# A gated mix of a state-space convolution and a GELU layer: start of the loads, time steps spread by a product, twelve warming products, due times from a table

## The chip, the core and the metric

The kernel runs on one core of a Trainium2 chip. The metric is the device time of the kernel in microseconds (us), the median of some runs. The core has a matrix engine (TensorE, PE in the profile; the loads of its weights are PEld), a vector engine (VectorE, DVE), a scalar engine (ScalarE, ACT), GpSimd (POOL), a queue that issues transfers (SyncE, SP), and 16 DMA engines. Each engine works through its own instructions in the order of the program and waits at semaphores for the others.

## The reference

```
dt = exp(log_dt);  A = A_re + i A_im;  B, C likewise          # 512 channels x 128 states
K[d, l] = Re sum_n C[d,n] * exp(dt[d] * A[d,n] * l) * dt[d] * B[d,n]     # 2048 taps
a = causal convolution of u with K (by FFT) + u * Dskip       # 2048 x 512
b = gelu(x @ w1 + b1) @ w2 + b2,  x = u                       # 512 -> 1792 -> 512
g = sigmoid(sum(x * gate_w))                                  # one value per row
out = g * a + (1 - g) * b
```

## The kernel before

The program has two parts. `front` makes three streams of work at once. `dense` is the GELU layer: 64 steps: two passes, one for each half of w1's columns, over 8 blocks of 256 rows, four steps to a block; in a step one or two groups f of 128 columns of w1 are multiplied with the rows (L904 to L906, three products of 256 columns for each of four parts, because each float is split in a high and a low part), ScalarE makes the GELU (L921) and the high part (L924), VectorE the low part (L931), and the output products with w2 follow (L947 to L950). `taps` computes the convolution's kernel: for four groups u of 128 channels and four chunks c of each it builds powers and waves on VectorE and ScalarE, contracts them on TensorE (L709, 16 groups of 128 small products), and applies a first stage of a transform (L428), whose results go to memory (L751). `signal` applies the first stage (L428, too) to the input. Then `conv` reads both back, multiplies them in the frequency domain (L1140, L1179), and writes the result (L1295 on).

What `front` does is created as tasks, each with an engine, a duration, a due time and the tasks that it depends on. `Plan.run` goes through them like a simulator with the planner's own durations: each time an engine is free it takes, among the tasks that are ready at that moment, the one with the lowest due time (a task that needs another table of ScalarE counts `TABLE` more). The instructions are then emitted in that order, which is the order in which each engine and each queue works on the chip. Before the change the due times are formulas of the step with tuned constants (`T_0`, `T_MLP`, `K_0`, `T_KG`, `D_...`).

At the start, SP loads the first block of x in two halves (L801), `log_dt` (L504), then the pieces of w1 and w2 of 256 KB each (L1008), the biases and `prm` (L538). Each half of x and each piece is split in a high part (L806 or L808) and a low one (L810). A hidden product needs both halves of x and its piece of w1, split. TensorE starts with `warm`: `N_WARM` products of a tile of zeros (L1025), then two products (L1029) that spread the row b2 and the row gate_w over the 128 partitions.

The time steps dt take this way: `log_dt` is loaded as 128 x 4, VectorE and ScalarE compute exp (L488 to L501), SP stores the result to memory (L508), and GpSimd's queue reads it back, spread over all partitions (L540), before VectorE multiplies the parameters with it (L546). With that multiplication the taps begin.

## Time and profile before

| | us |
|---|---|
| runs: median (lowest to highest of 3) | 510.12 (509.39 to 512.53) |
| the profiled execution's own time | 510.31 |
| its span in the profile | 508.3 |
| TensorE busy in the span | 500.2 |
| VectorE busy | 430.0 |
| ScalarE busy | 364.7 |

The profiled execution's time is its span and 2.01 us around it. Busy time of an engine is the union of its instructions. Rows of a timeline give start, duration, engine, line, operation, tiles and shapes, and in brackets the idle time before and what ended it.

### The profile page before, as it was taken

To read this page: it belongs to the slowest core of one execution; us is meant where nothing else is said; L and a number is where in the kernel's file an instruction comes from. 1 tells how busy PE (TensorE), PEld (TensorE's weight loads), DVE (VectorE), ACT (ScalarE), POOL (GpSimd) and SP (SyncE) were. 2 spreads that over 40 slices of the span, in tenths; PEclk is the share of its full clock that TensorE was granted. 3 is DMA by queue.
4 is the path that set the end of the run, shared out by engine and by line. 5 is a ranking of instruction groups with operands and counts; after the bars stand their busy time and mean duration, and the time that the engine had idled before them with its cause. 6 is when DMAs were issued, how large, how long until landed. Compare 5 with 4: busy or idle time off the path is not lost.

```text
span 508.3 us, 12156 instructions
## 1 busy us (share of the span) xinstructions
PE 500.2 (98%) x4792; PEld 382.8 (75%) x4792; DVE 430.0 (85%) x814; ACT 364.7 (72%) x631; POOL 39.6 (8%) x80
## 2 busy tenths in 40 slices
PE   9999999999999999999998999999999999999996
PEld 6998788898989888788887898998898832222452
DVE  5797999999999999999998989999950188777546
ACT  5799997889999599999766998738634455565300
POOL 1000000000000000001020010120010000231100
PEclk9999999999999999999999999999999999999999
DMA  8977597732558642789594233951478899989997
GB/s 269 327 250 269 156 258 236 225 128 66 149 120 260 193 165 64 207 241 239 142 269 139 86 54 59 218 119 29 144 179 206 201 368 401 376 300 399 324 339 294
DMA packets 81552, 107.60 MB, mean 212 GB/s; under 512 B 39396, under 2 KB 43880, under 8 KB 80952
## 3 DMA queue, kind: packets, MB, share of 16 engines
q1 hardware_dynamic: 74936, 82.81, 51.6%
q0 software_dynamic: 6176, 21.80, 16.1%
q10 hardware_dynamic: 384, 2.23, 1.3%
q8 instruction: 37, 0.61, 0.5%
q14 instruction: 19, 0.16, 0.1%
HBM read 61.19 MB, written 45.62 MB: 210 GB/s over the span
## 4 chain that ended last, share of the span: by engine, by line
PE 74%; ACT 16%; DMA 4%; SPq 3%; issue 2%; DVE 1%; DVEq 0%; POOL 0%; ACTq 0%; POOLq 0%
PE pk L709 10%; PE ph L904 8%; PE acc L947 7%; PE ph L905 7%; PE ph L906 7%; PE acc L948 7%; PE acc L950 7%; PE p2u L1140 5%; PE p2k L1140 5%; PE pa L1179 3%; PE pb L1295 3%; ACT ph L921 2%; PE ph L428 2%; ACT L921 2%; SPq L751 1%
## 5 line engine op out<-in xcount | busy, mean ns | idle before, releaser
L904 PE MATMUL ph<-xh,wh 128*128 128x256 f32 x448 | 129.4, 289 | 0.5 <-ACT attic L446 0.5
L905 PE MATMUL ph<-xlo,wh 128*128 128x256 f32 x448 | 128.1, 286 | 1.5 <-issue 1.5
L906 PE MATMUL ph<-xh,wl 128*128 128x256 f32 x448 | 127.9, 285 | 0.0
L904 PEld LDWEIGHTS ph<-xh,wh 128*128 128x128 f32 x448 | 86.4, 193 | 9.3 <-issue 5.4
L905 PEld LDWEIGHTS ph<-xlo,wh 128*128 128x128 f32 x448 | 86.5, 193 | 3.5 <-issue 1.7
L906 PEld LDWEIGHTS ph<-xh,wl 128*128 128x128 f32 x448 | 86.4, 193 | 0.0
L947 PE MATMUL acc<-wh,hh 128*128 128x512 f32 x209 | 84.2, 403 | 0.0
L948 PE MATMUL acc<-wl,hh 128*128 128x512 f32 x209 | 82.2, 393 | 0.0
L950 PE MATMUL acc<-wh,hl 128*128 128x512 f32 x209 | 81.8, 392 | 0.0
L921 ACT ACTIVATE ph<-ph,b1t 128x256 f32<-128x256 f32 x112 | 50.4, 450 | 38.9 <-PE ph L906 37.1
L709 PE MATMUL pk<-y,den 128*32 128x64 f32 x2048 | 61.4, 290 | 0.0
L709 PEld LDWEIGHTS pk<-y,den 128*32 128x32 f32 x2048 | 57.2, 136 | 3.3 <-issue 1.8
L931 DVE TENSOR_TENSOR hl<-ph,hh 128x512 fp32r<-128x512 f32 (+1 forms) x62 | 38.3, 620 | 22.6 <-ACT hh L924 22.2
L947 PEld LDWEIGHTS acc<-wh,hh 128*128 128x128 f32 x209 | 39.3, 188 | 17.4 <-issue 7.8
L950 PEld LDWEIGHTS acc<-wh,hl 128*128 128x128 f32 x209 | 39.3, 188 | 8.8
L671 DVE TENSOR_TENSOR y<-y,ea 128x64 f32<-128x64 f32 (+4 forms) x80 | 45.4, 567 | 0.1
L948 PEld LDWEIGHTS acc<-wl,hh 128*128 128x128 f32 x209 | 39.3, 188 | 6.4
L516 DVE TENSOR_TENSOR loft<-den,zz 128x256 f32<-128x256 f32 (+2 forms) x48 | 37.4, 778 | 0.5
L517 DVE TENSOR_TENSOR loft<-den,zz 128x256 f32<-128x256 f32 (+2 forms) x48 | 37.3, 776 | 0.0
L1148 ACT COPY k<-p2k 128x512 f32<-128x512 f32 x32 | 18.7, 586 | 25.4 <-issue 10.2
L684 DVE TENSOR_TENSOR y<-y,loft 128x2048 f32<-128x2048 f32 x16 | 36.6, 2288 | 0.2
L924 ACT CAST hh<-ph 128x512 fp32r<-128x512 f32 (+1 forms) x62 | 33.0, 533 | 2.4 <-PE acc L948 0.2
(200 smaller groups left out, 875.0 us busy)
## 6 DMA issues: line engine op xcount, KB each, us to landing
tk_d<-sk SPq DMA_DIRECT2D x32, 256.0 KB, 5.0
t_d<-sa SPq DMA_DIRECT2D x32, 256.0 KB, 5.1
tu_d<-attic SPq DMA_DIRECT2D x40, 128.0 KB, 2.8
attic<-in_xt_dram SPq DMA_DIRECT2D x16, 256.0 KB, 5.4
xh_d<-xh SPq DMA_DIRECT2D x8, 512.0 KB, 4.5
xl_d<-xlo SPq DMA_DIRECT2D x8, 512.0 KB, 5.0
attic<-in_xs_dram SPq DMA_DIRECT2D x16, 256.0 KB, 5.3
out_dram<-io SPq DMA_DIRECT2D x16, 256.0 KB, 3.3
```

Of the source, the lines that this page charges most:

```text
L516: vec(2 * m, lambda: vv.tensor_mul(t, a, br), due, [ka, *kb], [kt])
L671: nc.vector.tensor_mul(both(n, 64 - 3 * n, n), both(0, 64 - n, n), an)
L709: nc.tensor.matmul(pks[q][32 * j : 32 * j + 32, :, gg], x[:, r, :, ch], y[:, r, :, ch], start=(r == 0), stop=(r == 1), skip_group_check=True,)
L904: nc.tensor.matmul(p, h, xh[xk][:, d], start=(d == 0), stop=False)
L905: nc.tensor.matmul(p, h, xlo[xk][:, d], start=False, stop=False)
L906: nc.tensor.matmul(p, lo, xh[xk][:, d], start=False, stop=(d == 3))
L921: nc.scalar.activation(phs[q][:, n], phs[q][:, n], AF.Gelu_apprx_tanh, bias=b1t[:, f : f + 1])
L931: nc.vector.tensor_sub(lo, phs[q][:, 0:nf], hi.bitcast(F32))
L947: nc.tensor.matmul(a, h, wh[1][w], start=start, stop=False, skip_group_check=seeded)
L948: nc.tensor.matmul(a, h, wl[1][w], start=False, stop=False, skip_group_check=seeded)
L950: nc.tensor.matmul(a, l, wh[1][w], start=False, stop=stop, skip_group_check=seeded)
L1140: nc.tensor.matmul(out[64 * i : 64 * i + 64], w, x, start=True, stop=True)
```

## The change

- SP's first loads are the second half of x, w1[0] and the first half of x. `log_dt` goes to GpSimd's queue.
- For the first 128 channels dt isn't read back from memory: a 0/1 matrix (`some`, 32 x 128, new columns of `c1`, loaded by GpSimd's queue) is scaled by dt on VectorE, a product with ones on TensorE spreads it over the partitions, and VectorE copies it to `dtb`. The store to memory stays, for the other three groups.
- `N_WARM` is 12 instead of 8.
- The due times of all 1,539 tasks are replaced by the entries of a table, `DUES`, one for each task in the order of creation; they are ranks, not times. The formulas and their constants (changed, too) now set only the order of creation. The planner's idea of early transfers changes (1.5 times as long in its first 6.5 us, 2.6 us instead of 1.2 to the end of one on GpSimd's queue).

`conv` is not touched. Counted in the order of creation, the lowest entries of SP's loads are: second half of x 0, w1[0] 1, first half 2, w1[1] 4, w1[4] 6, w2[1] 7, w1[3] 13, b1 16, w1[2] 18, w1[5] 19, w1[6] 22, w2[6] 23, w2[0] 25, w2[2] 32, `prm` 53. GpSimd's queue: b2 0, `log_dt` 2, gate_w 3, `some` 8, c1 9. TensorE: warm 0, the product that spreads dt 3, the first hidden product 6, the one that spreads b2 26, the one for gate_w 33.

```diff
-T_0 = 36.21
-T_MLP = 409.57
-K_0 = 25.82
-T_KG = 357.09
+T_0 = 36.61
+T_MLP = 402.64
+K_0 = 24.02
+T_KG = 346.19
...
-TABLE = 21.3
+TABLE = 8.48
...
-N_WARM = 8
+N_WARM = 12
...
+DUES = """
+2 48 1704 7 63 0 8 101 3 31 2 0 9 1 25 4 7 18 32 13 55 6 75 19 64 22 23 16 3 0 3 1 0 26 460 580 33 1539 174
...
+"""
...
     c1 = np.tile(np.stack([er, ei], 2).reshape(32, 64), (4, 1))
+    some = np.arange(P)[:, None] == np.arange(P) // 4
+    c1 = np.concatenate([c1, some], 1)
...
-                dma = max(dma, at + 1.2) + t.done
-                end = dma + 1.2
+                dma = max(dma, at + 1.2) + t.done * (1.5 if dma < 6.5 else 1.0)
+                end = dma + (1.2 if p == "SP" else 2.6)
...
-            move(2, lambda: nc.sync.dma_start(x, logdt.rearrange(shape, c=4)), D_DT, [], ["dt"])
+            move(2, lambda: nc.gpsimd.dma_start(x, logdt.rearrange(shape, c=4)), -300, [], ["dt"], queue="GP")
...
-            move(2, lambda: nc.sync.dma_start(dt_d.rearrange(shape, c=4), r), -200, ["dt"], ["dt_d"])
+            move(2, lambda: nc.sync.dma_start(dt_d.rearrange(shape, c=4), r), D_SD, ["dt"], ["dt_d"])
+            some, scaled, ones = (x4[0:32, 0, k] for k in range(3))
+            pl.add("POOL", 0.1, lambda: nc.gpsimd.memset(ones, 1.0), -190, [], ["x4"])
+            move(16, lambda: nc.gpsimd.dma_start(some, c1[0:32, 64:192]), -190, [], ["x4"], queue="GP")
+            vec(
+                UW,
+                lambda: v.tensor_mul(
+                    scaled.rearrange("p (a b) -> p a b", b=4),
+                    some.rearrange("p (a b) -> p a b", b=4),
+                    r[0:32].unsqueeze(1).to_broadcast([32, 32, 4]),
+                ),
+                -190, ["dt"], ["x4"],
+            )
+            mm(
+                0.4, lambda: nc.tensor.matmul(pus[1][:, 0:UW], ones, scaled, start=True, stop=True), -190,
+                ["x4"], [("pu", 1)], tiled=True,
+            )
+            vec(UW, lambda: v.tensor_copy(dtb, pus[1][:, 0:UW]), -190, [("pu", 1)], ["dtb"])
...
-            move(
-                200, lambda: nc.gpsimd.dma_start(dtb, dt_d[:, sl].to_broadcast([P, UW])), t - 20 if u else -97,
-                ["dt_d"], ["dtb"], queue="GP",
-            )
+            if u:
+                move(
+                    200, lambda: nc.gpsimd.dma_start(dtb, dt_d[:, sl].to_broadcast([P, UW])), t - 20,
+                    ["dt_d"], ["dtb"], queue="GP",
+                )
...
-                lambda: nc.gpsimd.dma_start(c1t, c1),
+                lambda: nc.gpsimd.dma_start(c1t, c1[:, 0:64]),
...
+        for t, due in zip(pl.tasks, map(float, DUES.split()), strict=True):
+            t.due = due
         for t in pl.run():
```

## Rows read from the trace of the kernel before

**Rows 1.** The page: span, busy time by engine, TensorE's granted clock in 40 slices.

```profile
span 508.3 us, 12156 instructions
...
PE 500.2 (98%) x4792; PEld 382.8 (75%) x4792; DVE 430.0 (85%) x814; ACT 364.7 (72%) x631; POOL 39.6 (8%) x80
...
PEclk9999999999999999999999999999999999999999
```

**Rows 2.** Busy time by stretch: length, each engine's busy us (instructions), clock, DMA.

```profile
0.00:8.41 8.41, 7.42 (x20) 4.54 (x20) 2.61 (x9) 3.71 (x6) 2.29 (x10) 1.00 0.68 210
8.41:13.47 5.06, 5.06 (x24) 5.06 (x24) 4.20 (x13) 3.53 (x5) 0.00 (x0) 1.00 1.07 383
13.47:402.90 389.43, 386.74 (x4254) 337.51 (x4252) 349.14 (x676) 314.17 (x539) 26.01 (x52) 1.00 0.62 173
402.90:503.98 101.08, 100.99 (x498) 35.72 (x497) 73.18 (x117) 43.30 (x82) 11.32 (x18) 1.00 0.96 350
```

**Rows 3.** Timeline of TensorE, the first 14 us: start, us, line.

```profile
0.99 3.79 PE L1025 MATMUL acc<-dm 128*128 128x128 f32 x16 [0.99 <-POOL dm L1019]
4.71 2.06 PE L1029 MATMUL acc<-io,s 1*128 1x512 f32 x2
6.57 1.91 PE L1029 MATMUL pu<-io,s 1*128 1x512 f32 x2
8.41 0.58 PE L904 MATMUL ph<-xh,wh 128*128 128x256 f32 x1
...
13.06 0.42 PE L904 MATMUL ph<-xh,wh 128*128 128x256 f32 x1
13.27 0.36 PE L905 MATMUL ph<-xlo,wh 128*128 128x256 f32 x1
...
13.58 0.28 PE L904 MATMUL ph<-xh,wh 128*128 128x256 f32 x1
13.70 0.29 PE L905 MATMUL ph<-xlo,wh 128*128 128x256 f32 x1
```

**Rows 4.** Timeline of SP's queue, the first issues.

```profile
0.74 0.87 SPq L801 DMA_DIRECT2D attic<-in_xt_dram  x2
1.66 0.42 SPq L504 DMA_DIRECT2D dts<-in_logdt_dram  x1
2.13 0.91 SPq L1008 DMA_DIRECT2D sk<-in_w_dram  x2
```

**Rows 5.** Timelines of ScalarE, VectorE, SP and GpSimd: w1's first piece, then dt.

```profile
7.09 0.62 ACT L808 CAST wh<-sk 128x512 fp32r<-128x512 f32 x1 [2.05 <-DMA sk<-in_w_dram]
7.74 0.69 DVE L810 TENSOR_TENSOR wl<-sk,wh 128x512 fp32r<-128x512 f32 x1 [1.37 <-ACT wh L808]
10.28 0.16 DVE L501 TENSOR_TENSOR dts<-dts,dts 128x4 f32<-128x4 f32 x1
10.54 0.33 SPq L508 DMA_DIRECT2D dt_d<-dts  x1
15.65 0.54 POOL L540 DMA_DIRECT2D dtb<-dt_d  x1 [12.46 <-DMA dt_d<-dts]
24.51 0.68 DVE L546 TENSOR_TENSOR pr<-pr,dtb 128x512 f32<-128x512 f32 x1
```

**Rows 6.** Waits of TensorE over the whole span: total, times, longest.

```profile
PE ph L905 <- issue: 1.5, 1, 1.5
...
PE ph L904 <- ACT attic L446: 0.5, 1, 0.5
```

**Rows 7.** The chain that ended last, around the start of `conv`: start, us, what.

```profile
394.77 7.46 DMA tk_d<-sk
405.16 4.12 DMA cc<-in_c_dram
415.61 1.72 PE p2k L1140 x8
```

**Rows 8.** Timeline of TensorE: the first products of `conv` on the taps.

```profile
406.41 4.33 PE L1140 MATMUL p2k<-tk,pr 128*64 128x512 f32 x16
```

More of the change, by code (lines that the diff above doesn't have):

```diff
@@ L33 @@
 NB = 2 * NSB
-T_0 = 36.21
-T_MLP = 409.57
-K_0 = 25.82
-T_KG = 357.09
-U_0 = 33.4
-U_GAP = 11.32
-LAG = 11.52
-TABLE = 21.3
-D_KA = 14.92
-D_KP = -48.19
-D_S1 = -107.61
-D_EV = -129.31
-D_H = -67.42
-D_LO = -64.4
+T_0 = 36.61
+T_MLP = 402.64
+K_0 = 24.02
+T_KG = 346.19
+U_0 = 31.29
+U_GAP = 11.78
+LAG = 9.33
+TABLE = 8.48
+D_KA = 27.96
+D_KP = -53.16
+D_S1 = -145.63
+D_EV = -88.51
+D_H = -29.0
+D_LO = -57.06
 PS = (2, 3, 1, 2)
 N_ACC, N_H, N_PK, N_PU = PS
-D_SP = 5.83
+D_SP = -0.18
 MEM = (6, 2, 5)
 N_LD, N_HL, N_ST = MEM
-D_XS = 6.62
-DOTS_AT = (0, 1, 7, 14, 15, 18, 20, 21)
-N_WARM = 8
-T_EARLY, T_LOFT, T_DEN = 347.49, 497.61, 268.21
-Y_K, Y_U = 55.03, 39.32
-W_MLP = (-0.0864, -0.0266, 0.0054)
-W_KG = (-0.056, -0.0124, 0.0011)
-W_U = (-0.025, -0.1189, 0.003)
-D_MAG = -1.84
-D_ROT = 0.71
-D_CON = 2.06
-D_PHA = -0.1
-D_PRE = -2.18
-D_XL = -29.86
-D_COE = -3.15
-D_OUT = -38.48
-D_GW = 95.59
-D_DT = -103.6
-D_B2 = 15.56
+D_XS = 66.26
+DOTS_AT = (0, 1, 5, 14, 15, 18, 22, 23)
+N_WARM = 12
+T_EARLY, T_LOFT, T_DEN = 329.63, 507.38, 299.82
+Y_K, Y_U = 63.16, 44.06
+W_MLP = (-0.083, -0.0225, 0.0026)
+W_KG = (-0.0522, -0.0191, -0.0062)
+W_U = (-0.0367, -0.1236, -0.0019)
+D_MAG = -0.23
+D_ROT = 0.94
+D_CON = 0.61
+D_PHA = -0.67
+D_PRE = -3.2
+D_XL = -27.23
+D_COE = -2.87
+D_OUT = -34.38
+D_GW = 3.72
+D_W1 = 0.61
+D_PR = -94.5
+D_SD = -116.26
+D_B2 = 90.72
 N_LATE = 2
@@ L537, in prepare @@
             act_due = t + D_KA
-            move(600, lambda: nc.sync.dma_start(pr, prm[:, :, sl]), t - 20 if u else -97, [], ["pr"])
-            move(
-                200, lambda: nc.gpsimd.dma_start(dtb, dt_d[:, sl].to_broadcast([P, UW])), t - 20 if u else -97,
-                ["dt_d"], ["dtb"], queue="GP",
-            )
+            move(600, lambda: nc.sync.dma_start(pr, prm[:, :, sl]), t - 20 if u else D_PR, [], ["pr"])
+            if u:
[3 more added lines that the diff above has]
+                )
             v = nc.vector
@@ L824, in load_x @@
                 return [
-                    load(xt[b, :, 2 * h : 2 * h + 2].rearrange("p a b -> p (a b)"), due)
+                    load(xt[b, :, 2 * h : 2 * h + 2].rearrange("p a b -> p (a b)"), due + 2 * h)
                     for h in range(2)
@@ L1008, in dense @@
                         256, lambda f=f, r=r: nc.sync.dma_start(room[f][:, r], w_rows(f, r)),
-                        -99 + f + r * 1.5, [], [("room", f, r)],
+                        -99 + f + r * D_W1 if f + r else -299, [], [("room", f, r)],
                     )
@@ L1038, in dense @@
             move(2, lambda: nc.sync.dma_start(dm[0:P:32], dskip), -80, [], ["dm"])
-            split_x(0, x, -50)
+            split_x(0, x, -52)
             first = [
-                split_w(f, r, room[f][:, r], ("room", f, r), -50 + f + r * 1.5, (f, r) in W_DVE)
+                split_w(f, r, room[f][:, r], ("room", f, r), -51 + f + r * D_W1, (f, r) in W_DVE)
                 for f in range(FH)
```

55 rows, old and new, of the table DUES are left out of this document.

## The prediction

> **What bounds the kernel now.** I read the page first, then the stretches, then what stands between them. TensorE is busy 98% of the span, and no other engine over 85% [rows 1]. A busy share says little by itself, so the next question is whether the engine is also quick while it is busy. In the stretches [rows 2] it has hardly a gap: 386.74 of 389.43 us from the clock's rise to the end of `front`, and 100.99 of 101.08 us in `conv`. A hidden product of 256 columns follows the one before after 120 ns (13.58 to 13.70, [rows 3]), which is 2.1 columns per ns, near the higher of the clock's two levels, 2.4 GHz. So from 13.5 us to 504 us TensorE is the bound, nearly free of waits, and the change leaves its 490 us of products as they are. What can be won stands in four places:
>
> - the 8.41 us before the first hidden product [rows 2];
> - the stretch from 8.41 to 13.47 us, in which a product takes 213 ns start to start (13.06 to 13.27, [rows 3]): 1.2 columns per ns, the lower level of 1.2 GHz. The page's granted clock reads full all the way [rows 1], so here the pace of the products tells the clock, not that row;
> - the waits in `front`: 2.7 us in its long stretch [rows 2], of which one of 1.5 us that no semaphore explains and one of 0.5 us on ScalarE [rows 6];
> - the start of `conv`, where 16 products on the taps take 4.33 us [rows 8], against 1.72 us for 8 later on [rows 7], so 3.44 for 16: 0.9 us lost. The chain tells why: it runs through the store of the last taps (7.46 us), then through the load of a factor, cc [rows 7].
>
> From 8.41 us on, every step that I cost on TensorE counts fully, since there is no idle time that could take it in. What is made quicker on another engine counts only where TensorE waits for it.
>
> **The change part by part.** The sum is made against the profiled execution's 510.31 us, a span of 508.3 and 2.01 around it. The median of the runs is 0.19 below, so what I find is taken off about 510.2.
>
> *The first loads.* A hidden product needs three transfers of 256 KB: both halves of x and w1[0]. Their order changes, not their number, so that w1's piece comes before a half of x gives nothing by itself: the third to land still sets the start. What goes is the issue of `log_dt` ahead of the third, 0.42 us on SP, by which the third is issued at about 1.66 instead of 2.13 us [rows 4]. Behind its landing stand the same two steps as now: ScalarE's high part from 7.09, VectorE's low part from 7.74 to 8.43 us [rows 5], and the first product at 8.41 [rows 3]. The third lands up to 0.5 us earlier, if the DMA engines, which carry small transfers of GpSimd's queue at that time, let it. One more small transfer there (`some`) may take that back: between -0.5 and 0. I take -0.3, a first product at 8.1 us, as the issue time is sure and the landing isn't.
>
> *Warming.* Sixteen records (each product counts as two) take 3.79 us up to the b2 product's start [rows 3]; eight more at the recorded 213 ns or so are 1.7 us. The warming then ends at about 6.4 us. The b2 product, 1.86 us at the low clock (4.71 to 6.57, [rows 3]), ends at 8.3, beside the first hidden product's 8.1: the cover is the wait for the loads, and it is used up to the last tenths. The gate_w product (another 1.84 us, 6.57 to 8.41) has no room ahead of the first hidden product at the low clock. By its rank, 33 against 6, it stands behind as long as the planner thinks the hidden product ready; if it stands ahead, the first hidden product is at 10.1 us, 1.7 later than now. So this part costs between 0 and 1.7 us if the clock stays low, and nothing if it rises by then, since both spreads take half as long.
>
> *What warming is for.* The 24 records from 8.41 to 13.47 take 5.06 us [rows 2]; at 120 ns they take 2.9. If the clock is up by the first hidden product, that is -2.2 us, to be kept to the end, as no wait follows that could eat it. If it isn't, 0. The row shows a stubborn clock: TensorE was busy from 0.99 us without a gap of 0.2 us, and rose only at 13.4, after 5 us of products on the full array with data. Before that it had 3.7 us of full-array products of zeros and 3.7 us of products one row high [rows 3].
>
> The Trainium skill (TensorE: Matmul & The Clock Gate, Part 1, "What's actually happening") has it that the low clock is the default and that sustained activity of the array releases it. Taken plainly, that would have raised the clock ahead of 8.41 us already, and the trace disagrees: full pace came at 13.5. By the plain rule more warming gives the -2.2; by this row, in which work of just this kind stood ahead of 8.41 us and raised nothing, it gives 0.
>
> I take -2.2. The row does show that the clock rises under products that follow each other without a pause, and the warming now goes on for 1.7 us more, up to 2 us before the hidden products. But I hold this at little over even odds.
>
> *The product that spreads dt.* New on TensorE, 128 columns, 32 rows. The trace has no such product; the nearest are the warming products of 128 columns (two records, 0.43 us at the low clock, so about 0.21 at the high one) [rows 3]. A change between product shapes comes on top. Between 0 (ahead of the first hidden product) and 0.6: I take +0.3.
>
> *What it replaces.* Today dt is ready at 10.44 us, stored from 10.54, read back by GpSimd's queue from 15.65, and used at 24.51 [rows 5]: 14 us of which VectorE does nothing for dt. After the change VectorE adds a product and a copy of 128 elements; `log_dt` comes by GpSimd's queue behind b2, so its landing may be half a us later; ahead of it in rank are only loads. The taps may then begin at 13 to 16 us, when `prm` has landed, 8 to 11 us earlier. VectorE has the room: it is busy 2.61 of the first 8.41 us and 4.20 of the next 5.06 [rows 2]. But VectorE isn't the bound, so an earlier start of the taps is worth only what TensorE waits for them: the 0.9 us at the start of `conv`, whose chain hangs on the last taps' store, and part of the waits in `front`. From 13.47 to 402.90 us VectorE is busy 349 of 389 us [rows 2], so it does catch up part of the lead but not all. I take -0.8 of the 0.9: behind it the next to be late is the load of cc, which is issued after the loads of the taps and moves with them.
>
> *The table.* It changes the order of everything in `front`, and no row shows the new order; the ranks don't run with time, so I can't read the order off them. The work is the same; only waits and changes of shape differ. Bounds: all 2.7 us of waits gone, or as many more. The 1.5 us have no semaphore behind them [rows 6], so an order can't aim at them. Of the other 1.2 us I take half, -0.6. The store of dt remains, for the later groups, which have long to wait.
>
> Sum: -0.3 - 2.2 + 0.3 - 0.8 - 0.6 = -3.6, so 506.7 against the profiled time and about **506.6 us** for the median.
>
> **The rivals.**
>
> *The clock stays low* (or falls again in the time of the one-row products). Then -0.3 becomes 0 to +1.7 (the warming and the spreads are in the way), and -2.2 becomes 0: with +0.3 - 0.8 - 0.6 the sum is -1.1 to +0.6, so 509.0 to 510.8. For it: 7.4 us of busy but slow TensorE before 8.41 us. Against it: the longer run.
>
> *Everything comes together.* The clock rises (-2.2), the loads land 0.5 earlier, all waits of `front` with a cause go (-1.2), the 1.5 us doesn't come back, the start of `conv` is clean (-0.9), +0.2 for the spread: -6.1, so 504.1. If the new order also joins some of the 32 stretches of taps products with each other, it is less still; 503 is where I see the floor.
>
> *The order of the table is too tight*, the one that ends slower. The order is fixed when the program is built, with the planner's durations. A taps stretch of TensorE (16 of L709, 16 of L428) that the planner puts where its input is just ready makes TensorE stand still on the chip if VectorE or ScalarE is late by some tenths, with all the dense products queued behind it. Today's price for that is the 0.5 us of [rows 6]. With the -3.6 from the other parts, it takes 8 of the 32 stretches at 0.5 us to be back at no gain; if 20 wait, it is +10, less 3.6: about 516. For it: VectorE is busy 90% of `front`, so it is easily late. Against it: today's order comes from the same planner and has only 1.2 us of such waits in 389.
>
> *Nothing that counts*: the start needs all three loads anyway, dt's earlier arrival lies off the bound. That ends with the first rival, at 509 to 510.5.
>
> **How the numbers follow.** Forecast (505 to 508.5): 0.48. All together (502 to 505): 0.20. Clock low or nothing that counts (508.5 to 511.5): 0.22. Order too tight (511 to 518): 0.10. The likeliest gives 506.6. Leaving out a tenth at each end, the range is 503.0 to 511.5. One per cent is 5.1 us, about what a measurement of this kernel can tell from no change (the three runs before lie 3.1 us apart): faster than 505.0 is the second case and a little of the first, 0.25; slower than 515.2 is the far part of the last, 0.05; between them 0.70.
>
> **What would show it.** Right: the first hidden product at 8.0 to 8.4 us; 0.12 us from start to start of its products from the first on; the first multiplication of parameters by dt before 17 us; 16 products on the taps at the start of `conv` in about 3.5 us; TensorE's waits in `front` at 2 us or less; the last product of L1295 ending near 500.4 instead of 504. Wrong: 0.21 us from start to start until 12 us or later (the clock); a first hidden product at 9 us or later (the spreads in its way); waits of TensorE on VectorE or ScalarE before L709 or L428 that sum to over 3 us (the order). The forecast fails by much only through the last.

## The result and the profile after

| | before | after |
|---|---|---|
| median of the runs, us (lowest to highest) | 510.12 (508.90 to 512.53, 19 runs) | 512.20 (510.16 to 514.22, 19 runs) |
| ratio after to before, 95% interval | | 1.0037 (1.0022 to 1.0052) |
| the profiled execution's own time | 510.31 | 512.26 |
| its span | 508.3 | 510.4 |

The change made the kernel 0.37% slower. That is within the 1% to which the forecast gave 0.70, but its 506.6 us is wrong by 5.6 us, and the time lies 0.7 us above the end of the range. For the first 400 us the forecast came out near in its total, in part by luck; the time was lost in the 15 us behind them.

The page of the changed kernel: TensorE is busy 1.1 us less than before, in a span that is 2.1 us longer [rows 1].

```profile
span 510.4 us, 12182 instructions
...
PE 499.1 (98%) x4802; PEld 380.1 (74%) x4802; DVE 430.2 (84%) x816; ACT 363.0 (71%) x630; POOL 40.1 (8%) x82
```

The stretches of the changed kernel, cut where its work changes: before the first hidden product, the first weights, the rest of `front`, `conv` up to its first inverse product, the rest of `conv`. Columns as in [rows 2]; the three last are the granted clock, the share of time in which the DMA engines are busy, and their GB/s.

```profile
0.00:8.31 8.31, 6.08 (x26) 5.21 (x26) 3.58 (x10) 3.14 (x4) 3.49 (x13) 1.00 0.70 230
8.31:12.70 4.39, 4.39 (x37) 4.33 (x36) 2.41 (x9) 4.22 (x8) 0.00 (x0) 1.00 1.06 386
12.70:399.21 386.51, 386.12 (x4245) 335.25 (x4243) 350.98 (x682) 312.76 (x539) 24.46 (x50) 1.00 0.61 173
399.21:414.11 14.90, 11.21 (x40) 3.60 (x40) 4.55 (x9) 4.33 (x9) 0.86 (x1) 0.89 0.96 283
414.11:505.55 91.44, 91.32 (x459) 31.73 (x457) 67.82 (x108) 38.57 (x72) 11.31 (x18) 1.00 0.96 348
```

The same stretch of `conv` in the kernel before:

```profile
402.92:412.66 9.74, 9.69 (x42) 3.34 (x41) 5.37 (x9) 4.70 (x10) 0.00 (x0) 1.00 0.91 296
```

`front` ends at 399.21 us instead of 402.90 [rows 2]: 3.7 us are won there. The same work of `conv` then takes 14.90 instead of 9.74 us, so its first inverse product comes at 414.11 instead of 412.66, 1.45 us later. The other 0.65 us of the longer span lie further back, 0.5 of them behind TensorE's last product.

TensorE's timeline at that place, and below it the chain of work that ended last:

```profile
399.21 3.65 PE L1223 MATMUL p2u<-den,pr 128*64 128x512 f32 x16 [0.18 <-ACT io L1058]
406.17 5.69 PE L1223 MATMUL p2k<-tk,pr 128*64 128x512 f32 x16 [3.30 <-DMA tk<-tk_d]
412.25 1.08 PE L1223 MATMUL p2k<-tk,cc 128*64 128x512 f32 x4 [0.39 <-ACT k L1231]
...
414.11 1.09 PE L1262 MATMUL pa<-v,pr 64*64 64x512 f32 x8
```

```profile
382.64 2.05 ACT sk L817 x4
...
395.06 7.36 DMA tk_d<-sk
...
402.56 3.57 DMA tk<-tk_d
```

TensorE is ready for the taps at 402.9 and stands still for 3.3 us, where before it came at 406.41 without a wait for the first load [rows 8]. Read backwards, the chain says why: the first load of taps (402.56) goes out when the last of eight stores has landed (402.42), and that store left at 395.06. The kernel before had it issued at 394.77 and landed at 402.23 [rows 7]. The last taps are as late as ever, though TensorE had 3.7 us less to do in front of them.

At the start the reader sees the clock. The changed kernel's first products:

```profile
2.23 5.11 PE L1106 MATMUL acc<-dm 128*128 128x128 f32 x24 [2.23 <-POOL phase L846]
7.26 1.12 PE L1110 MATMUL acc<-io,s 1*128 1x512 f32 x2
8.31 0.39 PE L985 MATMUL ph<-xh,wh 128*128 128x256 f32 x1
8.54 0.27 PE L986 MATMUL ph<-xlo,wh 128*128 128x256 f32 x1
...
11.26 0.28 PE L985 MATMUL ph<-xh,wh 128*128 128x256 f32 x1
...
12.78 1.12 PE L1110 MATMUL pu<-io,s 1*128 1x512 f32 x2
14.11 0.48 PE L585 MATMUL pu<-x 32*128 32x128 f32 x2 [0.21 <-DVE x L577]
14.53 0.39 PE L985 MATMUL ph<-xh,wh 128*128 128x256 f32 x1
```

The b2 product takes 1.12 us, where it took 2.06 before, and from the second one on the hidden products follow each other after 0.12 us (24 of them from 8.31 to 11.26; before, 0.21 us each [rows 3]): the higher of the two levels, from the end of the warming on. The first multiplication by dt comes at 19.0 instead of 24.5 us [rows 5]:

```profile
19.00 0.67 DVE L627 TENSOR_TENSOR pr<-pr,dtb 128x512 f32<-128x512 f32 x1
```

TensorE's waits in the whole span, in the changed kernel. Of the waits of `front` [rows 6] none is left over 0.21 us; the 2.2 us stand at the very start, before warming:

```profile
PE p2k L1223 <- DMA tk<-tk_d: 3.3, 1, 3.3
PE acc L1106 <- POOL phase L846: 2.2, 1, 2.2
```

### The profile page after: what moved, and what is told of

Its sections match the earlier page's. It is cut to its first block, busy times and chain, and to the rows that moved or that the text cites. A ratio compares the mean times of both kernels' runs of the same rounds, so it can differ in the third digit from the quotient of the medians.

```text
span 510.4 us, 12182 instructions
## 1 busy us (share of the span) xinstructions
PE 499.1 (98%) x4802; PEld 380.1 (74%) x4802; DVE 430.2 (84%) x816; ACT 363.0 (71%) x630; POOL 40.1 (8%) x82
## 3 DMA queue, kind: packets, MB, share of 16 engines
q10 hardware_dynamic: 384, 2.23, 1.3%
## 4 chain that ended last, share of the span: by engine, by line
PE 92%; DMA 2%; SPq 2%; ACT 1%; DVE 1%; issue 0%; POOL 0%; DVEq 0%; POOLq 0%
PE pk L790 12%; PE acc L1028 10%; PE ph L985 10%; PE ph L987 10%; PE ph L986 10%; PE acc L1029 9%; PE acc L1031 9%; PE p2k L1223 6%; PE p2u L1223 5%; PE pa L1262 3%; PE ph L491 3%; PE pb L1378 3%; DMA tk_d<-sk 1%; SPq L832 1%; PE acc L1106 1%; PE acc L1310 1%
## 5 line engine op out<-in xcount | busy, mean ns | idle before, releaser
L985 PE MATMUL ph<-xh,wh 128*128 128x256 f32 x448 | 127.5, 285 | 0.0
L986 PE MATMUL ph<-xlo,wh 128*128 128x256 f32 x448 | 126.8, 283 | 0.0
L985 PEld LDWEIGHTS ph<-xh,wh 128*128 128x128 f32 x448 | 85.2, 190 | 6.6 <-issue 4.6
L986 PEld LDWEIGHTS ph<-xlo,wh 128*128 128x128 f32 x448 | 85.2, 190 | 2.0
L987 PEld LDWEIGHTS ph<-xh,wl 128*128 128x128 f32 x448 | 85.2, 190 | 0.0
L790 PE MATMUL pk<-y,den 128*32 128x64 f32 x2048 | 61.4, 290 | 0.0
L790 PEld LDWEIGHTS pk<-y,den 128*32 128x32 f32 x2048 | 57.2, 136 | 3.7 <-issue 1.4
```

The lines of the kernel that those rows point to most:

```text
L790: nc.tensor.matmul(pks[q][32 * j : 32 * j + 32, :, gg], x[:, r, :, ch], y[:, r, :, ch], start=(r == 0), stop=(r == 1), skip_group_check=True,)
L985: nc.tensor.matmul(p, h, xh[xk][:, d], start=(d == 0), stop=False)
L986: nc.tensor.matmul(p, h, xlo[xk][:, d], start=False, stop=False)
L987: nc.tensor.matmul(p, lo, xh[xk][:, d], start=False, stop=(d == 3))
```

## The experiments

**The theory** to be tested: `conv` starts by the chain of the last taps (first stage, four copies to `sk`, eight stores, first load), and what TensorE wins in front of it becomes a wait. **The rivals**: the table's order costs something elsewhere; the clock, which is granted at 0.89 behind the wait, is the loss; the extra warming does harm.

Each kernel's trace gives four places on that chain. Times in us; n is the number of runs; the ratio is to the kernel before on the same chip (medians 509.82 to 510.44). Two kernels were profiled a second time, and have two values.

| kernel | `front` ends | last taps landed | first p2k | first inverse | median (n) | ratio (95%) |
|---|---|---|---|---|---|---|
| before; again | 402.92; 402.59 | 402.23; 401.64 | 406.41; 406.07 | 412.66; 412.00 | 510.12 (19) | 1 |
| after; again | 399.21; 398.51 | 402.41; 402.18 | 406.17; 405.27 | 414.11; 412.91 | 512.20 (19) | 1.0037 (1.0022 to 1.0052) |
| a_stores | 400.25 | 399.39 | 404.48 | 411.62 | 509.14 (12) | 0.9996 (0.9978 to 1.0013) |
| a_stores_cc | 399.09 | 397.97 | 403.78 | 411.36 | 509.66 (12) | 1.0003 (0.9982 to 1.0025) |
| a_best | 399.02 | 396.46 | 402.56 | 410.87 | 509.32 (12) | 0.9981 (0.9966 to 0.9996) |
| a_taps | 401.17 | 407.61 | 410.46 | 418.85 | 516.23 (6) | 1.0133 (1.0105 to 1.0161) |
| a_all | 401.91 | 407.07 | 409.68 | 417.97 | 515.93 (6) | 1.0130 (1.0101 to 1.0159) |
| a_keep | 398.98 | 402.12 | 405.81 | 413.35 | 511.06 (12) | 1.0026 (1.0007 to 1.0044) |
| a_free | 398.86 | 402.99, not waited for | 403.82 | 412.86 | 510.38 (12) | 1.0008 (0.9991 to 1.0025) |
| a_wide | 398.97 | 396.75 | 402.46 | 410.01 | 509.13 (12) | 0.9975 (0.9955 to 0.9995) |
| b_wide | 402.01 | 395.77 | 405.50 | 411.43 | 509.65 (12) | 0.9989 (0.9965 to 1.0013) |
| a_warm8 | 398.87 | 402.24 | 405.60 | 413.24 | 511.98 (9) | 1.0051 (1.0032 to 1.0070) |
| a_formula | 420.76 | 417.59 | 424.24 | 430.18 | 525.43 (6) | 1.0303 (1.0272 to 1.0334) |
| b_warm12 | 401.56 | 400.56 | 405.04 | 410.97 | 507.91 (12) | 0.9959 (0.9943 to 0.9975) |
| b_stores_warm12 | 400.81 | after 394.9 | 404.29 | 410.70 | 507.36 (7) | 0.9958 (0.9941 to 0.9974) |
| b_best | 399.91 | after 392.4 | 403.39 | 409.32 | 507.30 (10) | 0.9950 (0.9934 to 0.9967) |
| b_pad | 401.25 | 400.41 | 404.74 | 410.67 | 510.07 (12) | 0.9979 (0.9956 to 1.0002) |
| b_pad2 | 403.62 | 402.67 | 407.10 | 413.03 | 509.36 (12) | 0.9973 (0.9951 to 0.9996) |

Kernels named a_ start from the changed kernel, those named b_ from the kernel before. The places are of one profiled execution each; the first hidden product alone came between 6.9 and 10.1 us in these profiles, and a median stands between 0.6 us under and 4.0 us over its kernel's profiled span. So a place is good to a us or so, and where two kernels differ by less, only the ratios speak.

**The last stores ahead of the other transfers.** In the changed kernel SP works off the eight stores with three loads of `tu` between them.

```diff
# a_stores: the eight stores of the last taps get the lowest due times
-            t.due = due
+            t.due = -1.0 if t in last else due
# a_stores_cc, besides: cc is loaded ahead of the taps
-            if n == 4:
+            if n == 0:
# a_best, besides: two of the last four copies to sk
-                    lambda: nc.scalar.copy(
+                    lambda: nc.vector.tensor_copy(
```

> The changed kernel; in SP's queue alone, the eight stores of the last taps are issued one behind the other, ahead of the four loads of the signal that stand between them now; all other engines keep their order. Theory A (the store of the last taps decides when conv starts): the last store lands some 5 us earlier than at 402.4, TensorE's wait of 3.3 us before the first product on the taps and the slow products behind it go, and the time falls by 3 to 6 us, to 506 to 509. Theory B (the order of the table costs elsewhere, and conv's start is late since its own loads and the transfer engines are slow): less than 1 us of difference.

> The changed kernel with the stores of the last taps ahead of the tu loads, and cc ahead of the taps' loads. Against the run with the stores alone (509.14, first inverse at 411.62): if TensorE's second stop in conv's start is the wait for cc behind four loads, the products behind the first eight come 0.3 to 0.5 us earlier and the time is 508.3 to 509; if the taps' own loads, which then come one issue later, are what counts, it is 509 to 509.8.

> The changed kernel with three edits on the chain of the taps: the eight stores of the last taps issued ahead of the tu loads, cc loaded ahead of the taps instead of behind four of them, and two of the four copies of the last taps on VectorE beside the two on ScalarE. The chain theory expects the last landing at 397 to 398.5 (after: 402.41), TensorE waiting under 0.5 us at the start of conv (after: 3.3), no stretch of low clock there, the first inverse product at 409.5 to 411 (after: 414.11), 505.5 to 508 us and a ratio of 0.990 to 0.996 to the kernel before. The rival (the clock falls in these products whatever TensorE waited for) keeps 0.89 there and expects 509.5 or more.

With the last taps 3.0 us earlier, the first inverse product came 1.3 to 2.5 us earlier than in the two profiles of the changed kernel, and the time fell by 0.4%: 1.0037 became 0.9996, back to the kernel before. cc made no difference that can be told. a_best reaches 0.9981. Its landing at 396.46 is the one that the theory wanted, and the granted clock stays 1.00, but the time is 1.3 us above the expected band. A new wait in its timeline is as long:

```profile
402.56 1.07 PE L1223 MATMUL p2k<-tk,pr 128*64 128x512 f32 x2
404.93 4.24 PE L1223 MATMUL p2k<-tk,pr 128*64 128x512 f32 x14 [1.29 <-DMA tk<-tk_d]
```

The first load was issued at 396.83 and landed at 402.52, the second at 404.89. The loads no longer wait for the stores, but they still take 5.7 us and more. The end of the chain isn't only an order of events.

**The last taps earlier on TensorE.** Groups 13 to 15 of L790 and the last first stage get the lowest due times; a_all joins this with a_best's edits.

```diff
-                mm(1.83, lambda g0=g0: products(g0), ...)
+                (last.append if g > 12 else id)(mm(1.83, lambda g0=g0: products(g0), ...))
```

> The changed kernel, but TensorE takes the contractions of the last three chunks (groups 13 to 15) and the last first stage as soon as the planner has them ready; the planner then moves group 13 and what follows on all engines, nothing ahead of it. SP's order of stores against loads stays the planner's. Theory A (conv's start hangs on the last taps): the lead that VectorE has until group 12 (4.5 us against the kernel before) is kept, the last store lands 2 to 4 us earlier than at 402.4, and the time falls by as much, to 508 to 510. Theory B (the loss lies elsewhere): within 1 us of the changed kernel's 512.2.

> The changed kernel with the contractions of the last three chunks taken as soon as they are ready, the last taps' stores ahead of the signal's loads, half of the last first stage's four copies given to VectorE, and the factor cc issued ahead of the loads of the taps. Theory A: each shortens the chain from the last contraction to conv's first product on the taps; the wait and the low clock behind it go, and the time falls to 505 to 507, below both kernels. Theory B: 511 to 513.

A miss that teaches: group 15 began 4 us earlier (372.0 instead of 376.1), but the last first stage 5 us later (386.6 instead of 381.4), and until then TensorE works on the dense layer's products without a gap. By the program the first stage takes its turn at a bank that the dense steps use, in the order of creation; that this held it back is read from the program and not tested. The last taps landed 5.2 us later than in the changed kernel, and the time rose by 4.9 us (1.0133 against 1.0037). With the edits above, that is the dose in both directions: the taps earlier, the time down; the taps later, the time up, while the end of `front` moves by 2.7 us at most.

**The clock in the wait.** Four products between the first signals and the first taps keep TensorE busy; their sums go nowhere.

```diff
+        fill = ps.tile([P, D], F32, tag="pa0", name="fill", bufs=1)
+        for _ in range(4):
+            nc.tensor.matmul(fill[0:64], mats[0][0][0][:, 0], us[0], start=True, stop=True)
         taps(0)
```

> The changed kernel with four products of 512 columns into an unused bank between conv's products on the signal and its first products on the taps, some 3 us of work that TensorE otherwise waits. Theory A with the clock as its second part (the wait itself is set by the store, but it also lets the clock fall, so that the 16 products behind it take 5.7 instead of 4.3 us): 1 to 2 us faster, 510 to 511. Theory A without the clock (the 5.7 us come from late loads): no change, or up to 0.5 us slower.

The granted clock of the same stretch is 1.00 instead of 0.89:

```profile
398.98:413.35 14.37, 13.53 (x48) 4.00 (x48) 6.07 (x12) 4.43 (x9) 0.86 (x1) 1.00 0.96 287
```

The stretch takes 14.37 us all the same, about the 14.90 and 14.40 of the two profiles of the changed kernel (clock 0.89 and 0.88), and the intervals of the ratios overlap. So the low clock there is no loss of its own that can be told; TensorE waits for the loads either way.

**The wait taken away.** The eight first loads read blocks of u, stored long before, in place of the taps.

```diff
-            nc.sync.dma_start(t2s[n], tk_d[ko[n]])
+            nc.sync.dma_start(t2s[n], (tu_d if n < N_TK else tk_d)[ko[n]])
```

> The changed kernel, but the eight first loads of tk in the last stage read the blocks of u in place of those of the taps (8 of the 32 blocks of taps are left out of the convolution); those were stored long before, so no product there waits for the last taps. All else stands. If the late landing is what took the lead: TensorE waits less than 0.5 us between its first product of the last stage and the first inverse product, the granted clock there is 0.98 or more, the first inverse product comes 9.7 us after the first product as in the kernel before, at 408.9 (after: 414.11), and the time is 506.0 to 508.0 us, 0.992 to 0.996 of the kernel before. If what was lost lies elsewhere (the clock, or something behind the last stage's start), it stays at 509.5 or more.

This was to be the proof, and it failed: 510.38 us, first inverse product at 412.86, where 408.9 was expected. SP's queue and TensorE there:

```profile
393.07 3.39 SPq L832 DMA_DIRECT2D tk_d<-sk  x3
396.56 5.49 SPq L1202 DMA_DIRECT2D tk<-tu_d  x4
```

```profile
403.82 1.07 PE L1223 MATMUL p2k<-tk,pr 128*64 128x512 f32 x2 [1.31 <-DMA tk<-tu_d]
406.92 3.69 PE L1223 MATMUL p2k<-tk,pr 128*64 128x512 f32 x14 [2.03 <-DMA tk<-tu_d]
```

Nothing held the first load back. It was issued at 396.56, 6 us earlier than in the changed kernel, and landed at 403.77, 2.35 us earlier, after 7.2 us; the second landed at 406.87, as late as with the wait (406.80). TensorE waited the same 3.3 us, in two pieces. The time did fall, from 1.0037 to 1.0008, with intervals that just touch; 0.992 to 0.996 was expected. So the theory in its first form, that the load is late since it waits for the store's end, holds for a part of the loss at most. What else could hold the loads back is the DMA engines, busy with what stands ahead. Their share speaks for it. The changed kernel, 388 to 403 us:

```profile
388.00:393.00 5.00, 5.00 (x42) 4.92 (x41) 0.69 (x1) 1.48 (x3) 0.00 (x0) 1.00 0.99 239
393.00:398.00 5.00, 5.00 (x31) 4.44 (x30) 0.69 (x1) 2.99 (x7) 0.86 (x1) 1.00 0.95 214
398.00:403.00 5.00, 4.69 (x25) 1.89 (x23) 1.12 (x2) 1.89 (x4) 0.86 (x1) 1.00 0.96 161
```

They are busy 0.95 to 0.99 of the time and move 161 to 239 GB/s, where the rest of `conv` gets 348 at 0.96. The stores write pieces of 256 bytes. **The second theory**: the DMA engines' time for these pieces is the bound at `conv`'s start.

**The same stores in larger pieces.** The last eight stores write their 256 KB each into whole rows of a block; eight transfers on GpSimd's queue, early on, fill the place that they leave. The cut shows the stores.

```diff
...
+                    if u == D // UW - 1:
+                        nc.sync.dma_start(
+                            tk_d[k0_order()[h]].rearrange("(p a) d -> p (a d)", a=2),
+                            sk[64 * n : 64 * n + 64, ss].rearrange("p s c j g -> p (s c j g)"),
+                        )
+                        return
```

> The changed kernel, but the eight stores of the last taps write the same 256 KB each into whole rows of one block, in pieces of 4 KB in place of 256 B (the taps of the last 128 channels end in the wrong places; eight transfers on GpSimd's queue fill their own place with taps of the first unit, early on). If the DMA engines' time for the small pieces is the bound at the start of the last stage: the stores land by 394 (in the changed kernel 402.4), TensorE waits less than 0.5 us before p2k, the first inverse product starts at 408.5 to 409.5, and the time is 506 to 508 us, 0.991 to 0.996 of the kernel before. If the pieces don't matter, the wait stays above 2 us and the time at 510 or more.

> The same eight stores with 4 KB pieces in the kernel before, with the same early transfers. TensorE ends the work in front at 402.6 to 402.9 there and did not wait for the taps, so by the theory nothing is won: first inverse product at 411.8 to 412.7, 509.3 to 510.3 us. If stores that land earlier help by themselves (a freer DMA for the rest of the last stage), 507 to 509.

In the changed kernel the stores land by 396.75 (394 was expected), TensorE finds the taps there, and the same stretch runs without the wait for them:

```profile
402.46 3.68 PE L1234 MATMUL p2k<-tk,pr 128*64 128x512 f32 x16
...
410.01 1.68 PE L1273 MATMUL pa<-v,pr 64*64 64x512 f32 x8 [1.55 <-DVE v L1260]
```

```profile
388.00:393.00 5.00, 5.00 (x42) 4.87 (x41) 0.69 (x1) 1.48 (x3) 0.00 (x0) 1.00 0.89 295
393.00:398.00 5.00, 5.00 (x32) 4.49 (x31) 0.69 (x1) 3.23 (x7) 0.85 (x1) 1.00 0.95 248
398.00:403.00 5.00, 4.82 (x27) 2.05 (x27) 1.12 (x2) 1.65 (x4) 0.85 (x1) 1.00 1.04 338
```

From 388 to 403 us the engines move 295, 248 and 338 GB/s in place of 239, 214 and 161. The ratio falls from 1.0037 to 0.9975, by about 3.2 us. The DMA packets in the traces say where it comes from: the eight stores are 8,192 packets of 256 bytes and 19.3 ns each, 9.9 us of the 16 engines' time; in pieces of 4 KB they are 512 packets of 219 ns, 7.0 us, which is 2.9 less. (The 161 GB/s of the last stretch is not theirs alone: there the small pieces make 0.31 of the share of 0.96, and packets of 2 KB of other transfers take 214 ns instead of 113 in the first of the three stretches; why isn't traced.) In the kernel before the same edit gives 0.9989 (0.9965 to 1.0013), nothing that can be told from no change, as expected: there TensorE comes 3.5 us later and finds most of the transfers done. The edit also loosens the dependence (a load waits for the store of its own block; the first was issued at 393.19, before the last landing), but a_free, with no dependence at all, got only half of this. The expected 408.5 to 409.5 for the first inverse product was missed by 0.5 us, and the time by 1.1, through a new wait of 1.55 us: VectorE starts its first product with the taps only at 406.87, when a store of `out` has landed:

```profile
406.87 0.69 DVE L1256 TENSOR_TENSOR v<-p2u,k 128x512 f32<-128x512 f32 x1 [6.62 <-DMA out_dram<-io]
```

That is the next thing to be late at this place, and again it is a transfer.

The Trainium skill (DMA: Bandwidth & Descriptors, Specifications) asks for at least 512 bytes in a transfer's pieces for the full rate. The trace agrees in direction: by the packets above, 16 engines would move 212 GB/s in pieces of 256 bytes and 299 in pieces of 4 KB. No run here has pieces of 512 bytes.

**The parts of the change.** Without the table (its due times from the formulas, with the changed constants), with 8 warming products in the changed kernel, with 12 in the kernel before, and these 12 with a_stores' edit or with all of a_best's:

```diff
# a_formula
-        for t, due in zip(pl.tasks, map(float, DUES.split()), strict=True):
-            t.due = due
# a_warm8: range(8); b_warm12, b_stores_warm12, b_best: range(12)
-                for n in range(N_WARM):
+                for n in range(8):
```

> The changed kernel without the table: due times by the formulas with the changed constants, all else as changed. If the table's order loses the taps' lead (theory A, the loss is in where it puts the contractions): the taps end earlier than at 381.4 and the time is 2 us or more below 512.2. If the lead is lost in any order, because ScalarE's and VectorE's work is what it is: within 1 us of it, or slower by waits that the table avoids.

> The changed kernel with 8 warming products instead of 12, in the same order. Theory A: what TensorE loses at the start (up to 2.2 us of low clock, if the clock rises late as in the kernel before) is taken out of its wait before conv's first product on the taps (3.3 us now), and the end doesn't move by more than 1 us, or comes earlier, if the shorter wait leaves the clock up. Theory C (TensorE's products are the bound throughout, as the prediction had it): 2.2 us slower.

> The kernel before with 12 warming products instead of 8, in the same order. Theory A: front ends on TensorE up to 2.2 us earlier, the last store of the taps doesn't move, TensorE waits for it, and the end doesn't come earlier: 0 to 1.5 us slower, the latter if the wait lowers the clock. Theory C: 2.2 us faster, to 508.

> The kernel before with 12 warming products and with the last taps' stores issued one behind the other, ahead of the signal's loads, all else in the same order. Theory A: now the 2.2 us of the early clock reach the end, and the 0.9 us lost at conv's start as well: 2 to 3.5 us faster than before, 506.5 to 508. Theory C: 2.2 us faster from the clock alone, the same as with 12 warming products alone.

> The kernel before with 12 warming products, the eight stores of the last taps first, cc first and two of the last copies on VectorE; none of the spread product or the table. The chain theory: here TensorE's own work ends at about 401 and the landing comes before that, so the edits on the chain bring little over the 507.4 to 507.9 of the runs with 12 warming products: 506.5 to 507.5. The rival (the chain still ends conv's wait here) expects 505 to 506.

a_formula is slow through waits in `front`, which the table doesn't have:

```profile
PE acc L1028 <- ACT hh L1005: 4.6, 3, 1.7
PE ph L491 <- DVE hl L1012: 3.5, 2, 2.8
...
```

It doesn't price the table against the old formulas, as their constants changed too. a_warm8 is level with the changed kernel, and its first hidden products run at the high clock as well, though it warms no longer than the kernel before: there the four extra products are worth nothing. In the kernel before, 12 instead of 8 gain 0.41%. That speaks against theory A as it was put, which had no gain here, and for C (508). The taps came earlier with it: the last store landed 1.1 to 1.7 us earlier than in the kernel before, at 400.56, and the first load at 403.32, 1.7 us before TensorE used it, so nothing took the gain away. The timeline shows a clock that rises and falls again:

```profile
0.99 5.34 PE L1025 MATMUL acc<-dm 128*128 128x128 f32 x24 [0.99 <-POOL dm L1019]
6.27 1.12 PE L1029 MATMUL acc<-io,s 1*128 1x512 f32 x2
7.23 1.02 PE L1029 MATMUL pu<-io,s 1*128 1x512 f32 x2
...
9.35 0.30 PE L904 MATMUL ph<-xh,wh 128*128 128x256 f32 x1
9.46 0.40 PE L905 MATMUL ph<-xlo,wh 128*128 128x256 f32 x1
...
12.86 0.30 PE L906 MATMUL ph<-xh,wl 128*128 128x256 f32 x1
```

Sixteen starts at the slow pace instead of 22 (18 in the second profile) are 0.2 to 0.6 us, not 2.2. What else differs is the pause of 1.5 us in the kernel before that no semaphore explains [rows 6]: it is gone here, but another wait, 0.5 us in the kernel before, has grown by 1.0 us:

```profile
PE ph L904 <- ACT attic L446: 1.5, 1, 1.5
```

TensorE idles 2.7 us from its 37th hidden record to the end of `front`, as in the kernel before (2.7 and 2.3 in its two profiles). So in this profile the pause isn't the gain; 1.0 us of it is there when that record starts, at 14.05 instead of 15.0. Two kernels were to tell clock and pause apart, with four products of 16 columns behind or ahead of the 8 warming products, and the kernel before and the changed one were profiled again (in b_pad the four disturb the sums of the output, so b_pad2 is the one to read):

```diff
+                for n in range(4):
+                    nc.tensor.matmul(acc[1][:, 0:16], dm, dm[:, 0:16], start=True, stop=True)
```

> The kernel before with 4 products of 16 columns behind its 8 warming products: as many instructions on TensorE as with 12 warming products, hardly any more work. If the pause of 1.5 us without a named releaser at 266.5 in the kernel before goes by the place of the instructions, it is gone or stands elsewhere here, and the time falls by up to 1.5 us (508.6 to 509.2) if the taps end earlier with it; the first one-row products stay at the low clock. If the gain of 12 warming products came from the clock alone, the time stays at 509.7 to 510.2.

> The kernel before with 4 products of 16 columns ahead of its 8 warming products: as many instructions as with 12, hardly more work. If the pause at 266.5 goes by the place of instructions, it is gone and the time is 508.3 to 509.3 with the first hidden products still at the low clock; if 12 warming products gain by the clock alone, 509.7 to 510.3.

> The kernel before, a second look. If the pause at 266.5 belongs to the program, it is there again, 1.4 to 1.6 us long within 1 us of that place; if it belongs to one execution, it is missing or elsewhere. About 508 to 512 us.

> The changed kernel, a second look. If the wait for the last taps belongs to the program, TensorE waits 2.5 to 4 us for the first tk load again, and the clock stands below 0.95 in the products behind it; the first hidden products run at the high clock from the first on. 510 to 514 us.

The second profile of the kernel before has the pause at the same place (it ends at 268.0 us, at 268.3 in the first):

```profile
PE ph L905 <- issue: 1.2, 1, 1.2
```

Neither b_pad nor b_pad2 has it, and in both the hidden products start at the low clock, for 26 and 24 starts (in b_pad behind a b2 product at full pace, 0.53 us from record to record from 5.28 us on: there, too, the clock rose and fell again). They gain 0.21% and 0.27%; the first interval includes no change, the second ends just below it. So what the pause is worth isn't settled, nor where all of the gain of 12 warming products comes from. The pause doesn't go by the number of TensorE's instructions alone: b_wide has as many as the kernel before, and no pause.

The traces hold a candidate that no run tests. Queue q8 of the page loads instructions, 16 KB at a time, 37 or 38 times in a run, and in most places at nearly the same counts of TensorE's matmuls and weight loads, so they seem to be TensorE's own. In both profiles of the kernel before, the load at 265.8 us comes 471 and 452 of these behind the last one; in no other kernel are two loads over 444 apart. TensorE stops 1.0 us after that load starts, so it may have waited for its instructions.

The second profile of the changed kernel shows the wait of 3.1 us for the taps again, at clock 0.88, in 510.75 us.

b_best is ahead of both kernels, 0.9950 (0.9934 to 0.9967), 2.5 us under the kernel before; the edits on the stores, cc and the copies add nothing that can be told to 12 warming products alone (0.9959; with the stores 0.9958), since TensorE came last there. Theory A expected more of the stores with the 12 products than of the 12 alone; this was C's case again. The best variant of the changed kernel, a_wide at 0.9975, isn't ahead of these.

## Why the prediction was wrong

**What held.** The clock up from the first hidden product, which was the doubtful step: the first 24 of them take 2.95 us (8.31 to 11.26) instead of 5.17 (8.41 to 13.58 [rows 3]), 2.2 less, as forecast. (The 24 records that the prediction reads in 5.06 us [rows 2] are 23 and the end of the gate_w product.) The spread of dt in 0.42 us (0.3), and 0.21 of waiting ahead of it. `front` shorter by 3.7 us, against -2.8 for the parts that lie in it (-0.3, -2.2, +0.3, -0.6); the rival of a table that is too tight did not happen.

**What held by luck.** The first hidden product came at 8.31 us (8.1 forecast), but not when its loads were in. What it needs was split by 6.67 us:

```profile
5.98 0.69 DVE L891 TENSOR_TENSOR xlo<-attic,xh 128x512 fp32r<-128x512 f32 x1
```

TensorE was still at its warming, which began at 2.23 instead of 0.99, as GpSimd filled its tile of zeros only at 1.94, and at the b2 product until 8.31. With 8 warming products (a_warm8) the first hidden product is at 6.87. And the parts of the 3.7 us are not the forecast ones. The prediction counted the gate_w product as free behind the first hidden product. It is a step that was moved out of cover: before, it ran while the loads were under way, 6.57 to 8.41 us [rows 3]; now it stands at 12.78 between hidden products, and the next product starts 1.33 us later, 1.12 of work and 0.21 of waiting. So at the 37th hidden record (14.53 us; before, 15.01), with dt's spread done, the lead is only 0.5 us. The stretches from there to the end of `front`, before and after:

```profile
15.01:402.92 387.91, 385.22 (x4241) 335.97 (x4239) 349.14 (x676) 313.02 (x537) 26.01 (x52) 1.00 0.62 172
```

```profile
14.53:399.21 384.68, 384.50 (x4240) 334.66 (x4239) 349.18 (x677) 311.00 (x536) 24.46 (x50) 1.00 0.61 172
```

Of the other 3.2 us, 2.5 are TensorE's idle time, 0.18 us (384.68 less 384.50) in place of 2.69, where -0.6 was taken; the pause of 1.5 us is among them, at which by the prediction "an order can't aim", and it is gone in every other kernel that was profiled. The last 0.7 us isn't traced further.

**The step that failed** is the one on which the whole sum rested: "From 8.41 us on, every step that I cost on TensorE counts fully, since there is no idle time that could take it in", and with it "no wait follows that could eat it". No idle time in the trace of before doesn't say how far the engine is from idling. The room could be read in that trace, and it was small: the first load of taps landed at 405.26, 1.15 us before TensorE used it at 406.41 (1.18 in the second profile). Behind it there was less: the second load landed at 406.47 and the fourth at 408.77, each within 0.1 us of its first use (406.52 and 408.81; 0.5 and 0.6 us in the second profile). So not even 1.15 us won in front could be kept in full unless the taps came earlier too. What the runs show in its place: 3.7 us won, 3.3 us waited.

**The term of `conv`'s start** was -0.8, and the stretch measured +5.2 on the profile (14.90 in place of 9.74 us); with the 3.7 us won in `front` that leaves the first inverse product 1.45 us later. Even the 0.9 us that the term draws on was not all there. In the second profile of the kernel before, the 16 products on the taps have no loss:

```profile
406.07 3.68 PE L1140 MATMUL p2k<-tk,pr 128*64 128x512 f32 x16
```

Against these 3.68 us the first profile's 4.33 [rows 8] lost 0.65, as TensorE met the second and fourth loads. The term supposed that taps that begin earlier also end earlier, and that VectorE's lead is only partly used up. They began 5.5 us earlier (8 to 11 forecast), but the lead was gone by the end: the wave y was ready 5.2 us earlier in group 8, 2.9 in group 13 and 0.7 us later in group 14, and group 13's products on TensorE came 5.9 us after their y, before 1.3. Meanwhile VectorE waits longer for the contractions. These waits from 320 to 399 us, after and before:

```profile
DVE pk L806 <- PE pk L790: 7.2, 4, 4.1
```

```profile
DVE pk L725 <- PE pk L709: 3.6, 3, 3.0
```

That the table's order loses the lead there is read from the trace and not shown by an edit: in the one that tried to change it, a_taps, the last first stage stood behind the dense products.

The prediction did name the store of the last taps and cc in that chain, and took the place for 0.9 us of TensorE's time to be won. It is the place where the DMA engines are nearly full (0.91 and 0.90 from 393 to 403 us in the kernel before), and of its rows none shows this stretch by itself. The experiments carry this part: larger pieces in the same stores take 3.2 us off the changed kernel and nothing that can be told off the kernel before; without the dependence alone, or with the clock held up, the stretch stays nearly as long (14.0 and 14.4 us, where the two profiles of the changed kernel have 14.9 and 14.4).

**The rule on the clock**: the prediction took -2.2. That is what the plain rule of the Trainium skill gives (TensorE: Matmul & The Clock Gate, Part 1, "What's actually happening"), by which sustained activity releases the low clock. The changed kernel agrees, with b2 spread at full pace at 7.26 us. The other kernels agree only in part: a_warm8's 16 records of warming, from 2.22 to 5.8 us, were enough, the same 16 from 0.99 to 4.7 us in the kernel before were not, and in b_warm12 the clock rose and fell again under full work.

**What stays open**: whether the late load of instructions made the pause, and what made it late; why the eight loads of taps land 0.3 to 1.3 us later than in the kernel before (from 405.2 to 412.2 and 406.1 to 412.8 in the two profiles, before 404.9 to 410.9 and 405.3 to 411.9) though the stores end only 0.2 and 0.5 us later; and the 0.65 us behind the first inverse product, whose sign is turned in the second profiles (95.9 us to the end, before 96.6).

## What to carry to other kernels

Before an engine's saved time is counted to the end, read at the next hand-over how long the data had been there when that engine came, for the first load and for those behind it: here 1.15 us for the first and under 0.1 us for the second and the fourth, and no more than that could be won without moving the producer. A queue of transfers that is busy 0.95 of the time can bound a stage although the engine in front of it shows no wait, so its share and its GB/s belong to the rows that are read. Here, taking the dependence away brought half of what larger pieces brought. And a step that is moved out of a covered stretch costs its full time, even where the engine does it faster there.

## What the runs showed of the hardware

- TensorE's clock rose by the end of the warming with zeros (b2's product in 1.12 us from 6.27, 7.26 and 5.82 us on in b_warm12, the changed kernel and a_warm8), stayed low through it in the kernel before (2.06 us from 4.71), and in b_warm12 fell again at 9.46 us, after two products one row high and ten full-size records, with no gap in TensorE's work, to come back at 12.86.
- In a stretch of 14.9 us with one wait of 3.3 us the granted clock was 0.89, with p2k records of up to 1,117 ns in place of 592; with the same 3.3 us in two waits, 1.3 and 2.0 us (a_free), it was 1.00.
- Eight stores of 256 KB took 9.9 us of the 16 DMA engines' time in pieces of 256 bytes (19.3 ns a packet) and 7.0 us in pieces of 4 KB (219 ns). With the small pieces the engines moved 161 to 239 GB/s at a share of 0.95 to 0.99, with the large ones 248 to 338.
- A pause of 1.2 to 1.5 us without a releaser stands at the same place of one program in two executions, and is gone in all variants of it that were profiled, one of them with as many instructions on TensorE. Both times it began 1.0 us after the start of a load of instructions, which came 471 and 452 matmuls and weight loads behind the last; the longest such distance elsewhere is 444.
